# Top-k attention and two MLPs on one core: queries loaded and x transposed once per visit, and a newly searched order

## The chip, the core and the metric

The kernel runs on one core of a Trainium2 chip. A core has five engines, each with its own instruction queue that is worked off in order: TensorE (PE) for matmuls, VectorE (DVE), ScalarE (ACT), GpSimd (POOL) and SyncE (SP), which here issues all DMA transfers; these run on 16 DMA engines that the core shares out among all transfers. The metric is the time of one execution in device microseconds; the median of some runs counts.

## The reference

Four batches of eight heads, 576 positions of 64 values. Attention keeps, for each query, the 32 largest scores; its output goes through two MLPs with 2048 hidden units.

```python
scores = scale * np.matmul(q, k.transpose(0, 1, 3, 2))
kth = np.partition(scores, -32, axis=-1)[..., -32:-31]
scores = np.where(scores >= kth, scores, -1e9)
attn = softmax(scores)                       # with 1e-9 added to the sum
x = matmul(attn, v) as (4 * 576) x 512
h = x @ moe_w_in;   y = softplus(h) @ moe_w_out
h = y @ moe2_w_in;  out = (h - np.tanh(h)) @ moe2_w_out
```

(softplus is written out in the reference as max(h, 0) + log1p(exp(-|h|)).)

## The kernel before, in words

**Numbers.** Everything that PE multiplies is split into two 16-bit halves, a high and a low one, and a product is three matmuls (high by high, high by low, low by high). So every operand is made by ACT (cast to the high half) and POOL or DVE (difference, the low half).

**Visits and tiles.** Attention goes by visits: a visit is one batch, one pair of heads and two of the four blocks of 128 query positions (`PLAN`, line 32). There are 32 visits. Each has four full tiles of 128 queries by 576 keys (two heads by two blocks), kind "n". In every second group of visits a fifth tile holds the 64 left-over queries of both heads, kind "l". That makes 128 full and 16 left-over tiles.

A visit's preparation: `visit_load` (line 1219) loads queries to `qraw`, keys to `kraw`, values to `v`, and the left-over queries to `ql`; `visit_prep_q` (1290) scales the queries, splits them into `qhl` and has a DMA transpose them into `qT`; `visit_prep_left` (1306) does this for the left-over queries through a zeroed buffer `zq`, in which each head has its own block, into `qlT`. Keys and values of a visit that comes again are stored as split operands to DRAM (`kd`, `vd`) and loaded from there.

A tile's way: `front` (1341) multiplies queries and keys on PE into PSUM (`s`), ACT copies that to `ssb`; DVE runs four MAX8 and three MATCH_REPLACE8 to find the 32 largest; ACT (exponential) and DVE or ACT (mask) make `x`, the unnormalized probabilities; ACT and POOL split them to `hl`; a DMA transposes these to `pT`; `back` (1442) multiplies them with the values on PE into `px`, ACT scales by the reciprocal sum into `x32`. When both heads of one block of queries are there, ACT casts `x32` to the high half in `xs`, POOL makes the low half, and a DMA transposes `xs` into the chunk's tile `xy`, the input of the first MLP.

**MLPs.** Four visits (the eight heads of two blocks) fill a chunk of 256 positions; there are eight of these, and two of 128 for the left-over positions. `mlp_step` does one eighth of an MLP for a chunk: PE makes `h` from `xy` and the weights, ACT, POOL and DVE make `g`, PE adds to `y`. The weights (names `whi`, `wlo`; the number behind tells which) are loaded as raw 32-bit words in pieces of 1 MB or 256 KB, partly into the places of later weights or free `xy` tiles, and converted by ACT, DVE and POOL during the first 200 us.

**What sets the order.** The kernel's functions only record operations. A planner (`Recorder.order`, line 570) then lays them out: it starts from ranks with random noise (`SEED`, `SIG`), plays the program through with prices for every operation (`price`, 340, `place`, 462), and adds the entries of the table `SHIFTS`, each of which moves operations of some engines in a stretch of time by random or fixed amounts. The order that comes out is what each engine's queue holds. For PE gaps that it foresees it adds matmuls without use (`idle`, 607), 128x256, in the trace at line 677. All recorded operations are issued from line 680, so the trace shows them all under that line.

**Buffers.** `al(tag, n, ...)` hands out n buffers of a name in turn: `NQT` = 2 for `qT`, `NXS` = 3 for `xs` (one block of queries each), `NX32` = 2 for `x32`, `NXX` = 3 for DVE's `x`, `NQR` = 1 for `qraw`.

Of the kernel before, what the change touches and what calls it, by code (L numbers as in the profile page):

```python
# [35 lines left out]
NQT = 2  # L36
NHL = 1
XE = 1
# [4 lines left out]
NOWN = 8  # L43
# [29 lines left out]
NXS = 3  # L73
# [5 lines left out]
SEED = 3785  # L79
# [5 lines left out]
SIG = 60  # L85
# [10 lines left out]
NXX = 3  # L96
# [25 lines left out]
PTC = 1600.0  # L122
SPC = 640.0

SHIFTS = (
# [6 lines left out]
    (9776, 35155, 55155, 400, "A"), (63973, 103704, 123704, 400, "PDAGS"), (27296, 1008651, 1068651, 1000, "PDAGS"),  # L132
# [8 lines left out]
    (75800, 448312, 508312, 100, "PDAGS"), (73125, 179938, 219938, 400, "PD"), (19493, 716429, 756429, 200, "PDAGS"),  # L141
    (72577, 458633, 518633, 200, "G"), (91158, 95592, 115592, 1000, "G"), (38484, 434008, 442008, 6000, "G"), (63646, 482912, 522912, 100, "A"),
    (52951, 193726, 213726, 200, "PDAGS"), (90708, 836742, 896742, 400, "A"), (72979, 149882, 157882, 200, "PDAGS"),
# [540 lines left out]
def topk_attention_two_mlps(  # L684
# [81 lines left out]
    def with_table(out, in_, func, **kw):  # L766
        op = nc.scalar.activation(out, in_, func, **kw)
        nc.after(op, table[0])
        table[1].append(op)

    zq = al("zq", 1, [P, 2, 2, 2, D], F16)
    nc.gpsimd.memset(zq, 0.0)


    tiles_ = al("tiny", 1, [P, 176 if OWN < 99 else 120], F32)
    used_ = [0]

    def tiny(n=1):
# [663 lines left out]
    def back(st):  # L1442
# [38 lines left out]
        if st is not it.sts[-1]:  # L1481
            return
# [487 lines left out]
```

## Time and profile before

| | us |
|---|---|
| median of three runs | 1121.09 (1120.64 to 1122.13) |
| profiled execution | 1124.62 |
| its span | 1122.9 |
| PE busy | 1000.7 (89%) |
| DVE busy | 929.0 (83%) |
| ACT busy | 904.3 (81%) |
| POOL busy | 776.6 (69%) |

The span is what the profiler saw between the first and the last instruction; 1.7 us of the profiled execution lie around it. Busy shares are means over stages that differ: PE's granted clock, for example, is at half speed for some of the time between 80 and 190 us and full from 200 us on, so the same matmul has two durations. Matmul records overlap, since matmuls are pipelined: the step from one to the next is shorter than the duration shown.

### The profile page before, as it was taken

How to read it: one execution, taken by the hardware profiler on the slowest of the kernel's cores; microseconds unless marked ns; L12 is line 12 of the kernel's file. 1: busy time of each engine (PE TensorE's matmuls, PEld its weight loads, DVE VectorE, ACT ScalarE, POOL GpSimd, SP SyncE). 2: the span in 40 equal slices, each digit the busy share in tenths (PEclk: the TensorE clock that was granted, in tenths of full speed). 3: DMA queues.
4: the chain of work that ended last, by engine and by line, in shares of the span. 5: the costliest groups of instructions: out<-in, count | busy, mean ns of one | idle time of the engine just before them, and what ended most of it. 6: DMA issues, size and time to landing. Idle time of an engine off the chain costs nothing.

```text
span 1122.9 us, 27775 instructions
## 1 busy us (share of the span) xinstructions
PE 1000.7 (89%) x9994; PEld 784.6 (70%) x9994; DVE 929.0 (83%) x2059; ACT 904.3 (81%) x1873; POOL 776.6 (69%) x1185
## 2 busy tenths in 40 slices
PE   2437645989999899999999999999999999999998
PEld 1323334877678767876799868976787789968965
DVE  4987899989999999999999999999999899410111
ACT  5987999899998998888999898998988777633422
POOL 5794246999889667768788676788876657543433
PEclk9998855999999999999999999999999999999999
DMA  9999999547777886556887755577566363200000
GB/s 255 292 256 269 292 250 225 124 129 143 139 151 187 166 169 146 86 97 126 191 183 136 140 116 104 78 124 166 131 122 107 72 117 61 52 4 20 1 11 19
DMA packets 323130, 153.13 MB, mean 136 GB/s; under 512 B 270256, under 2 KB 314288, under 8 KB 322992
## 3 DMA queue, kind: packets, MB, share of 16 engines
q1 hardware_dynamic: 322992, 151.36, 62.7%
q8 instruction: 78, 1.28, 0.5%
q14 instruction: 60, 0.49, 0.2%
HBM read 73.01 MB, written 15.37 MB: 79 GB/s over the span
## 4 chain that ended last, share of the span: by engine, by line
PE 55%; DVE 18%; POOL 7%; ACT 7%; DMA 6%; issue 6%; SPq 2%; POOLq 0%; ACTq 0%; DVEq 0%
PE h L680 24%; PE y L680 24%; DVE x L680 7%; DVE m L680 7%; PE px L680 4%; PE s L680 3%; SPq L680 2%; POOL hl L680 2%; DMA pT<-hl 2%; ACT ssb L680 1%; POOL wlo L680 1%; ACT x L680 1%; DMA kraw<-in_k_dram 1%; DVE xy L680 1%; DVE wlo L680 1%
## 5 line engine op out<-in xcount | busy, mean ns | idle before, releaser
L680 PEld LDWEIGHTS <-whi 128*128 128x128 f16 (+1 forms) x3994 | 372.6, 99 | 78.3 <-DVE whi L680 14.4
L680 PE MATMUL h<-xy,whi 128*128 128x256 f16 (+1 forms) x2560 | 395.6, 263 | 1.5 <-DVE xy L680 0.6
L680 PE MATMUL h<-xy,wlo 128*128 128x256 f16 (+1 forms) x1280 | 325.0, 263 | 0.0
L680 DVE MAX8 m<-x 128x8 f32<-128x576 f32 x432 | 314.5, 746 | 0.9
L680 POOL TENSOR_TENSOR hl<-x,hl 128x64 f16<-128x64 f32 (+1 forms) x288 | 213.1, 757 | 82.8 <-ACT hl L680 62.1
L680 PEld LDWEIGHTS <-wlo 128*128 128x128 f16 (+1 forms) x1986 | 195.3, 99 | 34.2 <-issue 8.1
L680 DVE MATCH_REPLACE8 x<-m,x 128x576 f32<-128x576 f32 x288 | 213.9, 744 | 0.0
L680 PE MATMUL y<-g,whi 128*128 128x256 f16 (+1 forms) x1280 | 198.9, 262 | 1.1 <-POOL g L680 1.1
L680 PE MATMUL y<-whi,g 128*128 128x512 f16 x576 | 193.7, 379 | 0.3 <-POOL g L680 0.3
L680 POOL TENSOR_TENSOR g<-r,g 128x512 f16<-128x512 f32 (+1 forms) x160 | 173.4, 1084 | 20.3 <-PE y L680 11.3
L680 PE MATMUL y<-g,wlo 128*128 128x256 f16 (+1 forms) x640 | 162.3, 262 | 0.0
L680 DVE SCALAR_TENSOR_TENSOR r<-h,hinb,r 128x512 f32<-128x512 f32 (+1 forms) x80 | 54.8, 687 | 115.8 <-ACT r L680 115.4
L680 PEld LDWEIGHTS <-g 128*128 128x128 f16 x864 | 81.6, 98 | 74.5 <-POOL g L680 1.4
L680 ACT ACTIVATE x<-ssb,nb,tiny 128x576 f32<-128x576 f32 x136 | 117.4, 865 | 5.6 <-DVE m L680 2.9
L680 PEld LDWEIGHTS <-pT 128*128 128x128 f16 (+1 forms) x2240 | 89.6, 102 | 46.1 <-issue 22.4
L680 DVE MAX8 m<-ssb 128x8 f32<-128x576 f32 x144 | 107.6, 747 | 14.9 <-ACT ssb L680 14.5
L680 PE MATMUL px<-vhl,pT 128*128 128x65 f16 (+1 forms) x2240 | 96.8, 197 | 24.9 <-ACT x L680 12.1
L680 PE MATMUL s<-kT,qT 128*128 128x288 f16 x512 | 91.7, 306 | 20.9 <-ACT ssb L680 11.5
L680 PE MATMUL y<-wlo,g 128*128 128x512 f16 x288 | 109.1, 379 | 0.0
L680 DVE MATCH_REPLACE8 x<-m,ssb 128x576 f32<-128x576 f32 x144 | 106.5, 740 | 0.0
L680 ACT CAST hl<-x 128x576 f16<-128x576 f32 x144 | 96.5, 670 | 3.7 <-DMA pT<-hl 3.4
L680 ACT COPY ssb<-s 128x576 f32<-128x576 f32 x144 | 91.2, 633 | 4.8 <-PE s L680 4.1
(154 smaller groups left out, 1597.5 us busy)
## 6 DMA issues: line engine op xcount, KB each, us to landing
whi<-in_moe_w_in_dram SPq DMA_DIRECT2D x11, 1023.0 KB, 6.5
whi<-in_moe_w_out_dram SPq DMA_DIRECT2D x7, 1023.5 KB, 7.2
vd<-vhl SPq DMA_DIRECT2D x16, 330.0 KB, 3.8
vhl<-vd SPq DMA_DIRECT2D x16, 330.0 KB, 3.5
kd<-kT SPq DMA_DIRECT2D x32, 160.0 KB, 2.3
kT<-kd SPq DMA_DIRECT2D x32, 160.0 KB, 2.9
xy<-in_moe_w_out_dram SPq DMA_DIRECT2D x18, 255.8 KB, 3.4
qraw<-in_q_dram SPq DMA_DIRECT2D x64, 64.0 KB, 2.6
```

The source lines that it names most:

```text
L680: fn(*a, **k)
```

## The change

- `visit_load`: the queries of both heads of a visit come in one transfer.
- `visit_prep_left`: the left-over queries lie in `zq` without the zero blocks; one cast and one subtraction on 128 rows instead of two each on 64 rows, and the transpose is half as long. `front` reads the smaller `qlT`.
- `back`: `xs` and `x32` hold both blocks of queries of a visit; one cast, one subtraction and one transpose per visit, after its last full tile.
- Buffers: `NQT` 2 to 1, `NXS` 3 to 1 (twice as large), `NX32` 2 (twice as large), `NXX` 3 to 4, `NOWN` 8 to 2.
- Planner: a plain transfer's time is its bytes by 300 instead of 330 per ns; new `SEED` and `SIG`, and a new table `SHIFTS` with 206 entries instead of 264.
- Branches that no setting used are taken out.

```diff
-NQT = 2
+NQT = 1
...
-NXS = 3
+NXS = 1
...
-SEED = 3785
+SEED = 1322
...
-SIG = 60
+SIG = 25.0
...
-NXX = 3
+NXX = 4
...
 SHIFTS = (
-    (86484, 682077, 832077, 6000, "G"), (43207, 851448, 891448, 6000, "S"), (65683, 300726, 308726, 400, "PDAGS"),
...
+    (14983, 315778, 335778, 1000, "A"), (37653, 130389, 150389, 6000, "G"), (79820, 1004060, 1154060, 2500, "PDAGS"),
...
-            return (770.0 if kb == 32 else 690.0 if kb == 16 else 550.0 if kb in (230, 232) else SPC), size / 330.0
+            return (770.0 if kb == 32 else 690.0 if kb == 16 else 550.0 if kb in (230, 232) else SPC), size / 300.0
...
-            for j in range(2):
-                nc.sync.dma_start(
-                    vi.q[:, j],
-                    q[b, h0 + j, 0 : NB * P, :].rearrange("(p t) d -> p t d", t=NB)[:, ts[0] : ts[0] + nt, :],
-                )
+            nc.sync.dma_start(
+                vi.q,
+                q[b, h0 : h0 + 2, 0 : NB * P, :].rearrange("h (p t) d -> p h t d", t=NB)[:, :, ts[0] : ts[0] + nt, :],
+            )
...
-        for j in range(2):
-            r = slice(j * SL, (j + 1) * SL)
-            f = vi.ql[r, :].unsqueeze(1).to_broadcast([SL, 2, D])
-            nc.scalar.copy(zq[r, 0, j], f)
-            nc.gpsimd.tensor_sub(zq[r, 1, j], f, zq[r, 0, j])
-        vi.qlT = al("qlT", 1, [P, 2, 2, P], F16)
...
+        f = vi.ql.unsqueeze(1).to_broadcast([P, 2, D])
+        nc.scalar.copy(zq[:, 0], f)
+        nc.gpsimd.tensor_sub(zq[:, 1], f, zq[:, 0])
+        vi.qlT = al("qlT", 1, [P, 2, P], F16)
+        nc.sync.dma_start_transpose(out=vi.qlT, in_=zq.rearrange("p r u d -> p (r u d)"))
...
-        if st is it.sts[0]:
-            it.x = al("xs", NXS, [P, 2, P], F16)
...
+        if st is it.sts[0] and it is it.all[0]:
+            x = al("xs", NXS, [P, 2, nt, P], F16, cap=2 * P)
+            x32 = al("x32", NX32, [P, nt, P], F32, cap=2 * P)
...
-        if st is not it.sts[-1]:
+        if st is not it.sts[-1] or it is not it.all[-1]:
             return
...
+        nc.scalar.copy(hi, x32)
+        nc.gpsimd.tensor_sub(lo, x32, hi)
...
+        nc.sync.dma_start_transpose(out=to, in_=it.x[0:rows].rearrange("p r i c -> p (r i c)"))
```

What the order becomes is seen best at three places. In the rows, a name is a tile with its number, `out<-in` and the shape. The line number is that of the recorder's call, 680 before and 667 after the change.

The first place is SP's queue ahead of the last transposes of x that the first chunk (`xy_0_125`, `xy_0_126`) needs. Before:

```order
L680 DMA qraw_75<-in_q_dram 128x128 x2
L680 DMA_TRANSPOSE qT_86<-qhl_85 128x8x128
L680 DMA whi_0_71<-in_moe_w_out_dram 128x2x2047
L680 DMA_TRANSPOSE xy_0_126<-xs_128 128x2x128
L680 DMA vhl_138<-vd_139 128x1320
L680 DMA_TRANSPOSE pT_121<-hl_120 128x9x128
L680 DMA wlo_0_72<-in_moe_w_out_dram 128x1023
L680 DMA xy_0_98<-in_moe_w_out_dram 128x1023
L680 DMA_TRANSPOSE xy_0_126<-xs_135 128x2x128
```

After:

```order
L667 DMA qraw_75<-in_q_dram 128x2x128
L667 DMA kT_113<-kd_115 128x640
L667 DMA_TRANSPOSE qlT_147<-zq_63 128x2x128
L667 DMA kT_81<-kd_139 128x640
L667 DMA_TRANSPOSE pT_120<-hl_119 128x9x128
L667 DMA wlo_0_72<-in_moe_w_out_dram 128x1023
L667 DMA_TRANSPOSE xy_0_126<-xs_128 128x4x128
L667 DMA_TRANSPOSE pT_124<-hl_123 128x9x128
L667 DMA whi_0_71<-in_moe_w_out_dram 128x2x2047
```

Two transposes of 128x2x128 have become one of 128x4x128, and a 1 MB load of weights (`whi_0_71`, 128x2x2047), ahead of them before, now stands behind. The query load is one row instead of two.

The second place is ACT's queue at the same point of the program. Before:

```order
L680 ACTIVATE whi_0_69<-whi_0_71,tiny_64 128x1024
L680 ACTIVATE x_0_129<-px_127,r_2_140 128x64
L680 CAST wlo_0_72<-xy_0_96 128x256
L680 CAST xs_128<-x_0_129 128x128
L680 CAST wlo_0_72<-xy_0_97 128x256
L680 ACTIVATE px_134,ss_88<-px_134 128x128
L680 CAST wlo_0_68<-y_78 128x512
L680 ACTIVATE r_0_130<-px_127,tiny_64 128x1
L680 ACTIVATE ssb_94<-ssb_94,m_109 128x576
L680 ACTIVATE x_1_136<-px_127,r_0_130 128x64
L680 ACTIVATE x_110<-ssb_94,nb_117,tiny_64 128x576
L680 CAST xs_135<-x_1_136 128x128
```

After:

```order
L667 CAST hl_119<-x_93 128x576
L667 ACTIVATE r_0_130<-px_127,tiny_64 128x1
L667 ACTIVATE x_110<-ssb_111,nb_121,tiny_64 128x576
L667 CAST wlo_0_72<-xy_0_96 128x256
L667 CAST wlo_0_72<-xy_0_133 128x256
L667 ACTIVATE x_1_141<-px_127,r_0_130 128x64
L667 ACTIVATE px_134,ss_108<-px_134 128x128
L667 ACTIVATE whi_0_69<-whi_0_71,tiny_64 128x1024
L667 CAST xs_128<-x_1_141 128x256
L667 CAST hl_123<-x_110 128x576
L667 ACTIVATE whi_0_69<-whi_0_71,tiny_64 128x1024
```

The casts of `xs` are one of 128x256 instead of two of 128x128; the cast of weights from `y` (`wlo_0_68<-y_78`) that stood between them comes later, and the split of one tile's probabilities more (`hl_119<-x_93`) stands ahead.

The third place is SP's queue where the queries of the visit after the 28th are transposed to `qT`, late in the program. Before:

```order
L680 DMA kd_217<-kT_81 128x640
L680 DMA out_dram<-r_158 128x512
L680 DMA v_74<-in_v_dram 128x2x256
L680 DMA vd_216<-vhl_103 128x1320
L680 DMA_TRANSPOSE qT_86<-qhl_85 128x8x128
L680 DMA_TRANSPOSE pT_124<-hl_123 128x9x128
L680 DMA v_74<-in_v_dram 64x2x64 x2
L680 DMA_TRANSPOSE pT_121<-hl_120 128x9x128
L680 DMA_TRANSPOSE xy_0_100<-xs_128 128x2x128
```

After:

```order
L667 DMA_TRANSPOSE xy_0_132<-xs_128 128x2x64
L667 DMA vd_217<-vhl_136 128x1320
L667 DMA_TRANSPOSE pT_124<-hl_123 128x9x128
L667 DMA_TRANSPOSE pT_120<-hl_119 128x9x128
L667 DMA_TRANSPOSE qT_86<-qhl_85 128x8x128
L667 DMA kT_81<-kd_207 128x640
L667 DMA kT_83<-kd_209 128x640
L667 DMA vhl_103<-vd_208 128x1320
L667 DMA_TRANSPOSE pT_124<-hl_123 128x9x128
```

Before, the transposes of queries go to `qT_86` and `qT_116` in turn; after, all go to `qT_86`, which the tiles of the visit ahead are still reading, so this row now waits for the last score of that visit, and two transposes of probabilities (`pT`) and a store of values stand right ahead of it.

## Rows read from the trace of the kernel before

**Rows 1.** The page: span, busy time by engine, PE's busy tenths in 40 slices

```profile
span 1122.9 us, 27775 instructions
...
PE 1000.7 (89%) x9994; PEld 784.6 (70%) x9994; DVE 929.0 (83%) x2059; ACT 904.3 (81%) x1873; POOL 776.6 (69%) x1185
...
PE   2437645989999899999999999999999999999998
```

**Rows 2.** Timeline of PE: start, duration, operation (the first chunk's first matmul)

```profile
188.35 0.60 PE L680 MATMUL h<-xy,whi 128*128 128x256 f16 x2
```

**Rows 3.** Busy time by engine in stretches; then PE clock, DMA share, GB/s

```profile
0.00:188.35 188.35, 90.87 (x626) 58.33 (x627) 153.47 (x356) 161.57 (x329) 108.45 (x156) 0.84 1.03 262
188.35:270.00 81.65, 73.59 (x729) 62.82 (x728) 78.01 (x170) 74.98 (x171) 77.02 (x123) 0.97 0.59 139
270.00:500.00 230.00, 221.69 (x2265) 175.61 (x2264) 226.81 (x513) 209.45 (x449) 175.67 (x272) 1.00 0.73 145
```

**Rows 4.** The same stretches, the planner's matmuls without use alone (line 677; PE, PEld)

```profile
188.35:270.00 81.65, 8.31 (x64) 6.06 (x64) 0.97 0.59 139
270.00:500.00 230.00, 5.61 (x43) 4.11 (x43) 1.00 0.73 145
```

**Rows 5.** Waits of ACT and DVE before 188.35 us: total us, times, longest

```profile
ACT wlo L680 <- DMA whi<-in_moe_w_in_dram: 7.4, 3, 4.1
ACT wlo L680 <- DMA wlo<-in_moe_w_out_dram: 4.9, 1, 4.9
...
DVE whi L680 <- ACT wlo L680: 15.5, 5, 10.7
```

**Rows 6.** Timeline of SP: start, time of issuing, transfer

```profile
171.96 0.81 SPq L680 DMA_DIRECT2D qraw<-in_q_dram  x2
174.05 1.24 SPq L680 DMA_TRANSPOSE qT<-qhl  x1
```

**Rows 7.** DMA issues: count, KB each, median us from issue to landing

```profile
qraw<-in_q_dram SPq DMA_DIRECT2D x64, 64.0 KB, 2.6
...
xy<-xs SPq DMA_TRANSPOSE x80, 2.4
...
qT<-qhl SPq DMA_TRANSPOSE x32, 3.3
out_dram<-r SPq DMA_DIRECT2D x4, 128.0 KB, 2.4
qlT<-zq SPq DMA_TRANSPOSE x16, 2.6
```

**Rows 8.** Groups by operation and shape: busy us, mean ns of one | idle before

```profile
L680 ACT CAST qhl<-qraw 128x512 f16<-128x512 f32 x32 | 19.7, 616 | 0.4 <-DMA qT<-qhl 0.3
L680 ACT CAST xs<-x 128x128 f16<-128x128 f32 x64 | 18.8, 301 | 0.3
...
L680 ACT CAST zq<-ql 64x128 f16<-64x128 f32 x32 | 9.4, 295 | 0.5
...
L680 POOL TENSOR_TENSOR xs<-x,xs 128x128 f16<-128x128 f32 x64 | 28.0, 439 | 19.5 <-ACT xs L680 19.0
...
L680 POOL TENSOR_TENSOR g<-r,g 128x256 f16<-128x256 f32 x32 | 21.4, 673 | 1.3
...
L680 POOL TENSOR_TENSOR zq<-ql,zq 64x128 f16<-64x128 f32 x32 | 14.2, 443 | 5.1 <-ACT zq L680 3.5
```

**Rows 9.** What the DMA engines moved from 0 to 188.35 us

```profile
DMA packets 60466, 49.44 MB, mean 262 GB/s; under 512 B 39968, under 2 KB 57379, under 8 KB 60451
```

**Rows 10.** Groups of ACT from 188.35 to 270 us

```profile
L680 ACT CAST zq<-ql 64x128 f16<-64x128 f32 x4 | 1.2, 300 | 0.1
L680 ACT CAST xs<-x 128x128 f16<-128x128 f32 x3 | 0.9, 292 | 0.0
```

**Rows 11.** Timeline of PE at full clock: start, duration, operation

```profile
197.58 0.38 PE L680 MATMUL h<-xy,whi 128*128 128x256 f16 x2
...
197.91 0.38 PE L680 MATMUL h<-xy,whi 128*128 128x256 f16 x2
```

More of the change, by code (lines that the diff above doesn't have):

```diff
@@ L42 @@
 OWN = 2
-NOWN = 8
+NOWN = 2
 OWN0 = 0
@@ L769, in with_table @@
         table[1].append(op)
-    zq = al("zq", 1, [P, 2, 2, 2, D], F16)
-    nc.gpsimd.memset(zq, 0.0)
-    tiles_ = al("tiny", 1, [P, 176 if OWN < 99 else 120], F32)
+    zq = al("zq", 1, [P, 2, 2, D], F16)
+    tiles_ = al("tiny", 1, [P, 164 if OWN < 99 else 120], F32)
     used_ = [0]
@@ L1198, in topk_attention_two_mlps @@
             else:
-                c = NG * GW - 2 * 2 * (NB + 1) * D * p
+                c = (NG - 1) * GW - 2 * 2 * (NB + 1) * D * p
                 x = wlo[2][:, c : c + 2 * 2 * (NB + 1) * D].bitcast(F32).rearrange("p (h t d) -> p h t d", h=2, t=NB + 1)
@@ L1346, in front @@
             prods = []
[L1347 to L1349 removed]
         ps = al("s", 1, [P, 2, 512], F32, pb)
[L1351 to L1372 removed]
         with nc.burst():
[L1374 removed]
+            if st.kind == "l":
                 for hf in range(2):
@@ L1378, in front @@
                             c = slice(j * SL, (j + 1) * SL)
-                            nc.tensor.matmul(ps[c, hf, 0:HS], vi.qlT[:, r, j, c], vi.kT[j][:, hf * HS : (hf + 1) * HS],
+                            nc.tensor.matmul(ps[c, hf, 0:HS], vi.qlT[:, r, c], vi.kT[j][:, hf * HS : (hf + 1) * HS],
                                              start=(r == 0), stop=(r == 1))
-                prods = []
-            for hf in range(2):
+            for hf in range(2 if prods else 0):
                 for i, (lhs, rhs) in enumerate(prods):
@@ L1458, in back @@
                 nc.tensor.matmul(o, st.pT[:, NB, c0:c1], vl[:, NB, 0 : D + 1], start=False, stop=True)
-        if st is it.sts[0]:
-            it.x = al("xs", NXS, [P, 2, P], F16)
-            if XE:
-                it.x32 = al("x32", NX32, [P, P], F32)
+        nt = len(it.all)
+        if st is it.sts[0] and it is it.all[0]:
+            x = al("xs", NXS, [P, 2, nt, P], F16, cap=2 * P)
+            x32 = al("x32", NX32, [P, nt, P], F32, cap=2 * P)
+            for u, i in enumerate(it.all):
+                i.x, i.x32, i.one = x, x32, x32[:, u, :]
         rows = P if st.kind == "n" else SL
@@ L1475, in back @@
             sc, src = r[0:rows, i : i + 1], o[:, 0:D]
-            if XE:
-                nc.scalar.activation(it.x32[0:rows, c], src, AF.Copy, scale=sc)
-            else:
-                nc.scalar.activation(it.x[0:rows, 0, c], src, AF.Copy, scale=sc)
-                nc.vector.scalar_tensor_tensor(it.x[0:rows, 1, c], src, sc, it.x[0:rows, 0, c], op0=ALU.mult, op1=ALU.subtract)
-        if st is not it.sts[-1]:
-            return
-        if XE:
-            if XE == 1:
-                nc.scalar.copy(it.x[0:rows, 0, :], it.x32[0:rows])
-            else:
-                nc.vector.tensor_copy(it.x[0:rows, 0, :], it.x32[0:rows])
-            nc.gpsimd.tensor_sub(it.x[0:rows, 1, :], it.x32[0:rows], it.x[0:rows, 0, :])
-        nc.sync.dma_start_transpose(
-            out=it.chunk.x.block(vi.p)[:, :, it.col : it.col + rows],
-            in_=it.x[0:rows].rearrange("p r c -> p (r c)"),
-        )
+            nc.scalar.activation(it.one[0:rows, c], src, AF.Copy, scale=sc)
+        if st is not it.sts[-1] or it is not it.all[-1]:
+            return
+        hi, lo = (it.x[0:rows, u].rearrange("p i c -> p (i c)") for u in range(2))
+        x32 = it.x32[0:rows].rearrange("p i c -> p (i c)")
+        nc.scalar.copy(hi, x32)
+        nc.gpsimd.tensor_sub(lo, x32, hi)
+        to = it.chunk.x.block(vi.p)
+        if st.kind == "n":
+            to = to[:, :, it.all[0].col : it.col + P].rearrange("p r (i c) -> p (r i) c", c=P)
+        else:
+            to = to[:, :, it.col : it.col + rows]
+        nc.sync.dma_start_transpose(out=to, in_=it.x[0:rows].rearrange("p r i c -> p (r i c)"))
     class Halves:
@@ L1714, in topk_attention_two_mlps @@
                 its.append(it)
+                it.all = its
             for h in range(2):
@@ L1723, in topk_attention_two_mlps @@
                     it.spec, it.chunk, it.col, it.sts = vspec, lc, (ch.b % 2) * SL, []
+                    it.all = [it]
                     st = ST()
```

45 lines of the change are left out of this document (9 added, 36 removed), and 118 rows, old and new, of the table SHIFTS.

## The prediction

> **What bounds the kernel now.** I read the page first, then cut the span into stages. The page gives the matrix engine (PE) 1000.7 us of the 1122.9 us span [rows 1], so only 122.2 us are open to any reordering, and the change takes no matmul away. The slices say where these lie: PE is at 2 to 7 tenths in the first seven slices and at 9 from slice 11 on [rows 1].
>
> The cut that matters is the first matmul of the first MLP on attention output, which starts at 188.35 us [rows 2]. I call it the MLP start. The windows [rows 3] give PE's idle time as window minus busy: 97.5 us before 188.35; 8.1 us from there to 270; 8.3 us to 500; what is left of the 122.2 us, 8.3 us, lies in the 623 us after that. To this belong the keep-warm matmuls that the planner puts into foreseen gaps: 8.3 us from 188.35 to 270 and 5.6 us from 270 to 500 [rows 4]; these count as busy but are of no use. So: 97.5 us before the MLP start, 30.3 us of idle and filler time (8.1 + 8.3 + 8.3 + 5.6) between it and 500, and nearly nothing later. From 500 on PE sets the time, and an edit that only makes ACT, POOL or the queues lighter there is worth nothing.
>
> Before the MLP start no single engine is full: DVE is busy 153.5 of 188.35 us, ACT 161.6, the DMA engines show a share of 1.03 at 262 GB/s [rows 3]. ACT's idle time there is ended mostly by weight loads (7.4 and 4.9 us in the two largest rows), DVE's by ACT (15.5 us in the largest) [rows 5]. The chain reads: load, ACT, DVE, and the load end is where the supply is exhausted.
>
> **The change part by part.**
>
> *Queries in one load.* 64 loads of 64 KB become 32 of 128 KB, same bytes. An issue costs SP about 0.4 us (0.81 us for two [rows 6]), so 32 × 0.4 = 12.8 us of SP. SP is not on the path for long stretches, so I take 0. Landing: 2.6 us for 64 KB; the nearest row for 128 KB is an output store with 2.4 us [rows 7]. So the landing changes by some tenths either way, and the load is issued long before its use, while the tiles of the visit ahead are worked on; without that cover it would be a tenth of a us or two per visit.
>
> *One transpose of x per visit.* 64 transposes of two blocks become 32 of four. SP saves 32 issues of about 1.24 us, the price of the transposes of queries [rows 6], again off the path. A four-block transpose is in the trace already, for the left-over queries: 2.6 us against 2.4 us for two blocks [rows 7]. The MLP start needs both tiles of a visit anyway, so merging costs it 0.2 us. On ACT, 64 casts of 301 ns [rows 8] become 32 of 128x256. No such form is there; between 301 ns for 128 columns and 616 ns for 512 [rows 8] a straight line gives 406 ns (bounds: the two ends). Saved: 64 × 0.301 − 32 × 0.406 = 6.3 us. On POOL, 439 ns for 128 columns and 673 ns for 256 [rows 8] give 64 × 0.439 − 32 × 0.673 = 6.6 us.
>
> *Left-over queries without the zero block.* 32 ACT casts of 295 ns on 64 rows become 16 on 128 rows, priced as the 301 ns cast: 4.6 us; on POOL 32 × 0.443 − 16 × 0.439 = 7.2 us [rows 8]. ACT is spared 10.9 us in all and POOL 13.8 us, spread over the span; only what falls before 500 us counts.
>
> *Term 1, the MLP start.* The order shows what stands in each queue ahead of the last transpose that the first chunk needs. DVE: 281 rows in both; one more first replacement, two more others and two more maxima (5 × 0.75 + 3 loads of match values) against two 1.3 us weight subtractions and three small rows: +0.5 us. ACT: the edits save 8 × 0.301 − 4 × 0.406 + 4 × 0.295 − 2 × 0.301 = 1.4 us, and what is moved past the point saves another 0.5 us: −1.9 us. SP and DMA: a 1 MB weight load, one 0.26 MB load, and one 0.26 MB transpose stand behind this point instead of ahead of it, two 0.16 MB reloads of keys ahead instead of behind: by shapes 47.75 MB instead of 48.99 MB, which agrees with the 49.44 MB moved by 188.35 us [rows 9]. At 262 GB/s 1.24 MB is 4.7 us. Gains do not add on parallel chains: all 4.7 us if the transfers set the start, at most 1.9 us if ACT does, nothing if DVE does. I take 3.3 us, midway between the first two, because the chain begins at the loads but ACT is the busiest engine.
>
> *Term 2, 188 to 270 us.* ACT is busy 75.0 and POOL 77.0 of 81.65 us [rows 3] and PE starves between them. Three x casts and four left-over casts on ACT lie in the stretch [rows 10]. A merged pair of x casts saves 0.196 us on ACT and 0.205 on POOL, a left-over pair 0.289 and 0.447, so ACT is spared 1.5 × 0.196 + 2 × 0.289 = 0.9 us and POOL 1.5 × 0.205 + 2 × 0.447 = 1.2 us, both on the path there: −1.0 us. *Term 3, 270 to 500 us.* ACT's 10.9 us, spread over the span of 1123 us, give 2.2 us for these 230 us, where ACT is at 91% [rows 3]; the rest of its waits are not PE's, so I take somewhat under half: −1.0 us (bounds 0 and −2.2).
>
> *Term 4, one buffer for transposed queries.* This is the only added wait. The next visit's queries may be transposed only when the last full tile of the present visit has been scored; SP stands still on that PE wait (by its listed waits in 26 of 32 cases; a wait on PE stood there in 16 before, for a buffer two visits old), with probability transposes queued behind it. Then PE waits for 1.24 us of issue [rows 6] plus 3.3 us of landing [rows 7], 4.5 us, unless it has work between. From the order, with 0.33 us for three 256-column matmuls [rows 11] and the other forms by their columns, the work between the two scores is under 4.5 us at three of the 27 boundaries after the MLP start: 4.4, 4.0 and 2.0 us. That is 0.1 + 0.5 + 2.5 = 3.1 us if nothing else holds PE there and every transpose goes out at once. I take +1.5 us, bounds 0 and 17 (below).
>
> A fourth x buffer on DVE removes no large wait: the largest that ends DVE's idle time is ACT's weight cast [rows 5], not a buffer. I take 0. The changed rate in the planner (it makes a plain transfer longer, 300 for 330 bytes per ns) and the new tables work only through the order.
>
> The sum is −3.3 − 1.0 − 1.0 + 1.5 = −3.8 us: span 1119.1 us, profiled execution 1124.62 − 3.8 = 1120.8 us, and since the median of the runs shown is 1121.09 us, 3.5 us under the profiled one, 1117.3, say **1117 us**.
>
> **The rivals.** *No net change.* Occupancy of the transfers need not be a bound; then term 1 is at most ACT's 1.9 us, and with DVE's 0.5 us of extra work and the longer transpose it nearly vanishes, while term 4 eats terms 2 and 3: 1119 to 1123 us, likeliest 1121. The share of 1.03 speaks against it, DVE's 95% from 188 to 270 us [rows 3] for it: an earlier start meets a second chunk that comes no earlier. The Trainium skill states this side as a rule ("Perfetto Trace Analysis", Identifying the Most-Contended Engine): transfers are to be judged by HBM utilization, not by the engines' occupancy. By that rule 262 GB/s is no bound, term 1 falls to ACT's share, and the sum to −2.4 us or less; no row here settles it. The same page (DMA Optimizations) says that splitting transfers lets some start sooner, which speaks against both merges; the rows price that at 0.2 us.
>
> *Slower, by the single query buffer.* If the transposes leave SP 3 us late on the average, held by what stands ahead in that queue, PE needs 7.5 us of work at each boundary, and eight of the 27 have less (4.4, 5.0, 6.2, 4.0, 7.4, 6.6, 2.0, 7.1): 17.3 us lost, −5.3 + 17.3 = +12 us, 1133 us. At 1.5 us late four fall short, 8.6 us, 1124 us. It decides from about 1.3 us of lateness. For it: SP's queue is in order, and PE is so full after 500 us that any stall is paid in full. Against it: the order leaves 8 us or more at most boundaries. Likeliest 1126.
>
> *A larger gain.* If the new order lets ACT wait less for loads (12.3 us in two rows [rows 5]) and the start comes 8 us earlier, and half of the 16.4 us of idle and filler time from 188 to 270 us goes too, it is −16 us, 1105 us; with half of both, 1113. Against it: the order holds 110 fillers instead of 108, so the planner sees as many gaps as before.
>
> **How the numbers follow.** About 0.2%, 2.2 us, is what a measurement can tell from no change. Forecast (1112 to 1118.8): 0.42. Larger gain (1103 to 1112): 0.13. No change: 0.19. Slower (1123.4 to 1133): 0.26. So faster 0.55, same 0.19, slower 0.26. The range of 8 in 10 leaves a tenth or less on either side: 1107 to 1128.
>
> **What would show it.** Term 1: the first h<-xy matmul at 185 us (183.6 to 188) and some 1.2 MB less moved by then. Terms 2 and 3: ACT near 893 us, POOL near 763 us, and idle and filler time from the start to start + 312 us at 28 us instead of 30. Term 4: PE or its weight loads waiting for qT<-qhl after 200 us, 1 to 3 us in all; over 8 us and the slower case has come. A start after 190 us, or PE under 9 tenths after slice 20, would make the forecast wrong.

## The result and the profile after

The changed kernel takes 1112.51 us (median of 4 runs, 1109.65 to 1113.47). Its ratio to the kernel before is 0.9912, 95% interval 0.9890 to 0.9933, so 0.9% faster: about 9 us, where 4 us were forecast. The profiled execution took 1111.59 us, the span in it is 1109.9 us. The page of after, against [rows 1]:

```profile
span 1109.9 us, 27484 instructions
...
PE 998.6 (90%) x9996; PEld 785.7 (71%) x9996; DVE 928.0 (84%) x2059; ACT 898.2 (81%) x1825; POOL 769.7 (69%) x1136
...
PE   2446749989889999999999999999999999999998
```

The engines' sums have hardly moved: PE 2.1 us less, DVE 1.0, ACT 6.1, POOL 6.9. The span of the profiled execution is 13.0 us shorter. Part of that is the profiled execution of before, which lies 3.5 us above its median; the one of after lies 0.9 us under its own.

The gain has one place. The timeline of PE (start, duration, operation) has the MLP start, the first product of the first MLP, here, where [rows 2] had 188.35:

```profile
172.24 0.63 PE L667 MATMUL h<-xy,whi 128*128 128x256 f16 x2
```

It comes 16.1 us earlier, and 3.1 us of that are given back by the end (16.1 − 13.0). One profiled execution of each kernel stands behind these numbers. By the medians the gain is 9 us and not 13, and where in the span the 4 us between the two belong isn't known. The windows, cut at the start, 81.66 us and 230 us behind it as in [rows 3], show both. The columns are PE, PEld, DVE, ACT, POOL busy, then PE's granted clock, the DMA share and GB/s:

```profile
0.00:172.24 172.24, 87.15 (x622) 56.63 (x623) 152.67 (x352) 156.94 (x316) 105.70 (x144) 0.88 1.05 279
172.24:253.90 81.66, 75.47 (x725) 64.14 (x724) 76.28 (x177) 76.55 (x168) 79.03 (x119) 0.96 0.55 144
253.90:483.90 230.00, 217.83 (x2210) 172.23 (x2209) 221.93 (x496) 204.40 (x430) 171.95 (x261) 0.99 0.69 145
483.90:1109.90 626.00, 618.18 (x6445) 492.71 (x6442) 477.17 (x1038) 460.30 (x914) 413.02 (x614) 1.00 0.47 94
```

Read the DVE column of the first line, the third of the five. DVE does the same work before the start as before (152.67 us against 153.47), but in 172.24 us and not in 188.35. Its idle time there fell from 34.9 to 19.6 us, which is 15.3 of the 16.1 us. The waits of DVE before the start (total us, times, longest) say which idle time went. First those of before that [rows 5] does not show, then those of after:

```profile
DVE m L680 <- ACT ssb L680: 6.8, 4, 2.8
DVE wlo L680 <- ACT wlo L680: 5.7, 2, 4.5
```

```profile
DVE whi L667 <- ACT wlo L667: 12.2, 3, 10.0
...
DVE m L667 <- ACT ssb L667: 1.2, 3, 0.7
DVE wlo L667 <- ACT wlo L667: 1.2, 1, 1.2
```

DVE waits for ACT 13.4 us less in these three groups: 3.3 and 4.5 for casts of weights (the rows of `whi` and `wlo`), 5.6 for copies of scores. ACT, in turn, stood before weight loads for 15.5 us: the 12.3 us of [rows 5] and a third row. After, one group of such waits is left; the wait of 4.9 us for a W_out load is gone:

```profile
ACT wlo L680 <- DMA whi<-in_moe_w_out_dram: 3.2, 3, 1.4
```

```profile
ACT wlo L667 <- DMA whi<-in_moe_w_in_dram: 6.2, 2, 4.7
```

Sums of waits don't say which wait made which; the order of time does. One place in the kernel before can be followed from a load to DVE (start, duration, operation; the bracket: idle time before it, and what ended it):

```profile
88.12 1.33 ACT L680 CAST wlo<-wlo 128x1024 f16<-128x1024 bf16 x1 [4.89 <-DMA wlo<-in_moe_w_out_dram]
89.48 1.23 DVE L680 SCALAR_TENSOR_TENSOR wlo<-wlo 128x1024 int32<-128x1024 int32 x1 [4.54 <-ACT wlo L680]
```

ACT stands before a load that hasn't landed, and DVE, next in line, before ACT's cast: 4.5 of the 15.3 us. The longest wait for a copy of scores has another cause. PE had waited for transposed keys, so the scores themselves came late:

```profile
77.90 1.12 PE L680 MATMUL s<-kT,qT 128*128 128x288 f16 x4 [4.56 <-DMA kT<-khl]
79.72 0.76 DVE L680 MAX8 m<-ssb 128x8 f32<-128x576 f32 x1 [2.78 <-ACT ssb L680]
```

So late loads are one cause among several of the idle time that went.

Behind the start nothing is gained in these two executions. The planner's keep-warm matmuls (line 664 now, against [rows 4]; PE and PEld) in the two stretches:

```profile
172.24:253.90 81.66, 9.65 (x76) 7.27 (x76) 0.96 0.55 144
253.90:483.90 230.00, 4.94 (x25) 2.61 (x25) 0.99 0.69 145
```

Idle and filler time of PE in the 312 us behind the start is 6.2 + 12.2 + 9.7 + 4.9 = 33.0 us; it was 30.3.

### The profile page after: what moved, and what is told of

The parts are those of the page before. It is cut to its first block, busy times and chain, and to the rows that moved or that the text cites. A ratio compares the mean times of both kernels' runs of the same rounds, so it can differ in the third digit from the quotient of the medians.

```text
span 1109.9 us, 27484 instructions
## 1 busy us (share of the span) xinstructions
PE 998.6 (90%) x9996; PEld 785.7 (71%) x9996; DVE 928.0 (84%) x2059; ACT 898.2 (81%) x1825; POOL 769.7 (69%) x1136
## 4 chain that ended last, share of the span: by engine, by line
PE 58%; DVE 15%; ACT 10%; POOL 7%; issue 5%; DMA 4%; SPq 0%; ACTq 0%; POOLq 0%; DVEq 0%
PE h L667 26%; PE y L667 24%; DVE m L667 6%; DVE x L667 5%; PE px L667 4%; PE s L667 4%; ACT ssb L667 2%; ACT x L667 2%; POOL hl L667 2%; POOL wlo L667 1%; ACT wlo L667 1%; ACT whi L667 1%; DMA pT<-hl 1%; ACT hl L667 1%; ACT r L667 1%
## 5 line engine op out<-in xcount | busy, mean ns | idle before, releaser
L667 POOL TENSOR_TENSOR hl<-x,hl 128x512 f16<-128x512 f32 (+1 forms) x288 | 217.3, 771 | 77.5 <-ACT hl L667 63.5
L667 PEld LDWEIGHTS <-wlo 128*128 128x128 f16 (+1 forms) x1986 | 195.4, 99 | 39.1 <-DVE wlo L667 11.8
L667 DVE MAX8 m<-ssb 128x8 f32<-128x576 f32 x144 | 107.3, 745 | 10.7 <-ACT ssb L667 10.0
L667 POOL TENSOR_SCALAR r<-r,gsb 128x512 f32<-128x512 f32 (+1 forms) x80 | 52.6, 658 | 66.3 <-ACT g L667 65.8
```

Of the source, the lines that this page charges most:

```text
L667: fn(*a, **k)
```

## The experiments

All fourteen kernels in one table. "Start" is the first product of the first MLP, "DVE" its busy and idle time before that, GB/s the rate of the transfers there, "behind" the span less the start. The ratios are to the kernel before, which ran beside each with medians of 1120.97 to 1122.20 us; differences between two ratios are good to some 0.3%, 3 us. The changed kernel itself did not run beside the experiments. The columns from "start" on are of one profiled execution each.

| kernel | ratio to before, 95% | median us | start | DVE busy, idle | GB/s | behind |
|---|---|---|---|---|---|---|
| before | 1 | 1121.09 | 188.35 | 153.5, 34.9 | 262 | 934.6 |
| changed | 0.9912 (0.9890 to 0.9933) | 1112.51 | 172.24 | 152.7, 19.6 | 279 | 937.7 |
| forms_undone | 1.0017 (1.0002 to 1.0032) | 1122.02 | 172.51 | 153.5, 19.0 | 278 | 946.9 |
| xs_undone | 0.9986 (0.9967 to 1.0005) | 1120.05 | 173.21 | 153.3, 19.9 | 277 | 944.7 |
| q_undone | 0.9939 (0.9916 to 0.9962) | 1114.54 | 172.41 | 152.2, 20.2 | 279 | 941.4 |
| max_twice | 0.9991 (0.9970 to 1.0012) | 1119.12 | 177.67 | 159.0, 18.7 | 271 | 939.1 |
| early330 | 0.9983 (0.9968 to 0.9997) | 1120.80 | 179.09 | 152.7, 26.4 | 268 | 940.4 |
| search330 | 1.0002 (0.9982 to 1.0022) | 1120.70 | 176.63 | 151.5, 25.1 | 271 | 941.8 |
| x3 | 1.0296 (1.0269 to 1.0323) | 1153.39 | 178.19 | 154.9, 23.3 | 270 | 974.8 |
| x3_again | 1.0045 (1.0026 to 1.0064) | 1126.87 | 176.19 | 154.5, 21.7 | 273 | 947.9 |
| early300 | 1.0071 (1.0053 to 1.0089) | 1129.91 | 195.33 | 156.2, 39.1 | 254 | 930.9 |
| before_search300 | 1.0089 (1.0065 to 1.0112) | 1131.63 | 181.91 | 154.6, 27.4 | 263 | 948.3 |
| order_only | 1.0547 (1.0519 to 1.0575) | 1180.87 | 187.10 | 154.5, 32.6 | 257 | 994.7 |
| old_order | 1.1038 (1.1008 to 1.1068) | 1236.03 | 191.91 | 153.8, 38.2 | 256 | 1038.8 |

The theories at the outset: A, the searched order closes VectorE's gaps before the start; B, the merged instructions do it by lighter engines, as the terms of the prediction have it; C, the fourth x buffer does it.

In most of these kernels the planner's order is replaced by a stored place for every step; a step is issued at its place, or as soon behind it as all that it depends on has been issued:

```diff
-            done = self.order(margin)
+            done = self.given()
```

### forms_undone: the three merged forms taken apart, order kept

Each pair is recorded as one step, so that it keeps its place in the order. The lines that do this are left out here, and so is the order of the dimensions of `xs`, which follows the pairs:

```diff
-            nc.sync.dma_start(vi.q, q[b, h0 : h0 + 2, ...])
+            for j in range(2):
+                nc.sync.dma_start(vi.q[:, j], q[b, h0 + j, ...])
...
-        nc.scalar.copy(hi, x32)
-        nc.gpsimd.tensor_sub(lo, x32, hi)
-        nc.sync.dma_start_transpose(out=to, in_=it.x[0:rows].rearrange("p r i c -> p (r i c)"))
+        for u in range(nt):
+            nc.scalar.copy(it.x[0:rows, u, 0], it.x32[0:rows, u])
+        for u in range(nt):
+            nc.gpsimd.tensor_sub(it.x[0:rows, u, 1], it.x32[0:rows, u], it.x[0:rows, u, 0])
+        for u, i in enumerate(it.all):
+            nc.sync.dma_start_transpose(out=to[:, :, i.col : i.col + rows], in_=it.x[0:rows, u].rearrange("p r c -> p (r c)"))
...
-        nc.scalar.copy(zq[:, 0], f)
-        nc.gpsimd.tensor_sub(zq[:, 1], f, zq[:, 0])
+        for r in half:
+            nc.scalar.copy(zq[r, 0], f[r])
+        for r in half:
+            nc.gpsimd.tensor_sub(zq[r, 1], f[r], zq[r, 0])
```

> The changed kernel with its order, its four x buffers and its single qT and xs buffers kept step for step, but the three merged forms taken apart again where they stand: two loads of queries per visit, two casts, two subtractions and two transposes of x per visit, two casts and two subtractions of the leftover queries. Theory A (the searched order closes VectorE's gaps before the first W_in product; the forms weigh little): MLP start within 2 us of 172.2 us, time within 2 us of 1112.5. Theory B (the lighter ScalarE, GpSimd and DMA queue do it, the terms of the prediction): MLP start 3 to 16 us later, 175.5 to 188 us, and the time up by 3 us or more. Theory C (the fourth x buffer): no change, 1112.5.

The start did not move (172.51 us), which speaks against B as a theory of the start. Yet the whole gain is gone, 1122.02 us. B had a time like this, but none of the theories had a loss behind an unmoved start. The windows of this kernel (columns as above):

```profile
172.51:254.17 81.66, 74.23 (x707) 62.68 (x706) 75.22 (x172) 75.66 (x167) 77.20 (x119) 0.95 0.54 138
254.17:484.17 230.00, 215.48 (x2170) 168.55 (x2167) 217.98 (x489) 203.31 (x438) 173.95 (x273) 0.99 0.71 145
484.17:1119.40 635.23, 625.01 (x6507) 497.36 (x6505) 478.94 (x1050) 468.14 (x949) 422.76 (x643) 1.00 0.49 93
```

Behind the start PE needs 946.9 us and not 937.7: 6.0 us more idle time (32.2 against 26.2) and 3.2 us more busy time. PE issues the same instructions in the same order in both, so they can be set side by side. Of the 3840 products `h<-xy` the 251st comes 2.3 us later than in the changed kernel, the 501st 4.9, the 1251st 7.0, the 2001st (at 715 us) 10.0, the last 9.5: a loss in small pieces up to some 700 us, and none behind that. Among PE's waits behind 172 us the one for the transposed probabilities grew most, from the first line (the changed kernel) to the second (this one):

```profile
PE px L667 <- DMA pT<-hl: 2.4, 4, 0.8
```

```profile
PE px L1119 <- DMA pT<-hl: 6.5, 8, 1.5
```

### xs_undone and q_undone: one of the forms each

The edits are the second part of the diff above (xs_undone) and the first (q_undone).

> The changed kernel in its order, with the x step of a visit taken apart again: two casts, two subtractions and two transposes back to back instead of one each (32 more instructions on ScalarE, GpSimd and the DMA queue each). All three forms apart cost 9.5 us behind an unchanged start. If the transposes are what costs (each is a long issue on the queue, and the pT transposes behind it come later): 6 us or more of the 9.5, near 1119. If ScalarE and GpSimd time by itself costs, 32 times some 0.1 us each: 1 to 3 us, 1114 to 1115. MLP start within 1 us of 172.2 in both.

> The changed kernel in its order, with the load of queries of a visit taken apart into two again (32 more issues on the DMA queue, no other engine). If issues on the queue cost by themselves (32 times some 0.6 us, of which a part delays a transpose behind): 3 us or more, 1115 to 1119. If only the transposes and casts of x cost: within 1 us of 1112.5. MLP start within 1 us of 172.2.

The x step costs 0.74% when undone (0.9986 against 0.9912), about 8 us; the load of queries 0.27%, 3 us, which is as large as the uncertainty and decides between neither of its expectations. The 8 us are in the range that was expected if the transposes cost, not in the 1 to 3 us for ScalarE's and GpSimd's own time; over the whole span ACT is busy 1.2 us more than in the changed kernel (899.4 against 898.2) and POOL 2.0 (771.7 against 769.7). That the transposes' issues are the cause is still not shown: casts, subtractions and transposes were undone together. Behind 172 us PE's matmuls wait for pT nearly as before (2.8 against 2.4 us) and for ScalarE's score copies more (11.2 against 7.8 us). But PE also waits in its weight loads of `pT`. With these counted, the wait for transposed probabilities grows from kernel to kernel. In the views of `pT` from 172 us on, this line reads, for the changed kernel, q_undone, xs_undone and forms_undone (us, times):

```profile
  DMA pT<-hl: 5.7, 8
  DMA pT<-hl: 8.0, 11
  DMA pT<-hl: 9.9, 15
  DMA pT<-hl: 17.2, 21
```

These transposes stand in the same queue as the added issues, so this fits the transposes' side; waits of weight loads can overlap matmuls, and not all of them are lost time.

### max_twice: does DVE set the start now?

Shortened; the two maxima are one step of the order:

```diff
-            return lambda: nc.vector.max(m[:, 8 * i : 8 * i + 8], src)
+            for _ in range(2 if i == 0 and 1 <= st.i <= 12 else 1):
+                nc.vector.max(m[:, 8 * i : 8 * i + 8], src)
```

> The changed kernel in its order, with the first row maximum of twelve of the sixteen score tiles ahead of the first W_in product taken twice (12 more VectorE instructions of 0.74 us, 8.9 us in all, nothing else). If VectorE's own work with its few gaps sets the MLP start now: start 7 to 9 us later, 179 to 181 us, and the time up by 5 to 9 us. If bytes, ScalarE or the loads set it (the terms of the prediction): the start moves by 3 us or less.

```profile
0.00:177.67 177.67, 89.67 (x622) 57.28 (x623) 159.02 (x364) 158.70 (x316) 106.51 (x144) 0.88 1.03 271
```

Twelve more maxima make DVE 6.4 us busier before the start, the start comes 5.4 us later, and the median 6.6 us (9 us by the ratios). That lies between the two expectations (7 to 9 us, 3 us or less), nearer to the first. So DVE with its gaps sets the start for the greater part. It is not the fullest engine there: ACT is busy 156.9 of the 172.24 us of the changed kernel and DVE 152.7. No run added work to ACT, so whether ACT sets the start as much is not known. The stretch behind the start is 1.5 us longer than in the changed kernel: the shift isn't made up for by the end.

### early330: the old price of transfers, up to the start

Theory D: the planner of before, at 330 bytes per ns, puts ScalarE's casts ahead of loads that land later on the chip. Here only the steps ahead of the first product are laid out anew, with the changed kernel's priorities and the old price; each engine passes over a step whose transfer has not landed by the plan.

> The changed kernel with its instructions and buffers; only the order of the steps up to the first W_in product is laid out again with the old price of transfers (330 bytes per ns), behind it the order of the changed kernel. Theory D: loads land later than this order assumes, MLP start at 174 to 182 us instead of 172, time 1114 to 1121. Rival (price is of no weight, buffers and instructions are): start within 2 us of 172, time within 2 us of 1112.5.

```profile
ACT wlo L1108 <- DMA whi<-in_moe_w_in_dram: 6.5, 3, 3.6
ACT wlo L1108 <- DMA whi<-in_moe_w_out_dram: 4.6, 3, 2.5
```

```profile
DVE whi L1108 <- ACT wlo L1108: 12.3, 5, 9.0
DVE m L1108 <- ACT ssb L1108: 7.6, 6, 3.5
```

Start and time are as D expected: 6.9 us later, and 0.7%, 8 us, slower. ACT's waits for weight loads are back from 6.2 to 11.1 us, and DVE's wait for score copies from 1.2 to 7.6 us. But most of the second did not come from the first. The two longest of DVE's waits for score copies, 5.7 of the 7.6 us, in order of time:

```profile
52.72 1.14 PE L1108 MATMUL s<-kT,qT 128*128 128x288 f16 x4 [2.00 <-DMA qT<-qhl]
54.64 0.76 DVE L1108 MAX8 m<-ssb 128x8 f32<-128x576 f32 x1 [3.54 <-ACT ssb L1108]
...
96.26 0.58 ACT L1108 CAST wlo<-h 128x512 f16<-128x512 f32 x1 [1.50 <-PE h L1108]
101.51 0.76 DVE L1108 MAX8 m<-ssb 128x8 f32<-128x576 f32 x1 [2.19 <-ACT ssb L1108]
```

At 54.64 the scores came late, because PE had waited for transposed queries. At 101.51 ACT had waited for PE, and then had other work ahead of the copy. Neither stands right behind a late load. So the run shows that, with the same instructions and buffers, the order ahead of the start alone is worth 8 us and works through DVE's idle time (26.4 against 19.6 us). It doesn't show theory D's mechanism. Nor does it show that the price is the reason: the same laying out at 300 was not run for the changed kernel, so the way of laying out may itself cost what was lost.

### early300: the new price in the kernel before, up to the start

The same with the kernel before and its own priorities.

> The kernel before, with its own instructions and buffers. Only the order of the steps up to the first W_in product is laid out again: the same priorities as before, each engine passing over a step whose transfer, priced at 300 bytes per ns in place of 330, has not landed; nothing is searched, and behind the first W_in product the order is that of before. Theory D (before loses its time where ScalarE, in order, stands before a load that lands later than its plan assumed: 7.4 us for three W_in loads and 4.9 us for one W_out load before the start, and VectorE behind it): MLP start at 172 to 179 us instead of 188, ScalarE's waits for weight loads before the start down from 12.3 to under 7 us, time 1107 to 1115. Rival (the earlier start needs the fourth x buffer or the new instructions): start at 184 us or later, time 1118 or more.

The start came later, 195.33 us, and not earlier. The timeline of PE (the bracket: idle time before it, and what ended it) shows why:

```profile
180.95 1.11 PE L1125 MATMUL px<-whi 128*128 128x128 bf16 x8 [6.17 <-DVE whi L1125]
...
194.40 1.11 PE L1125 MATMUL px<-whi 128*128 128x128 bf16 x8 [7.07 <-DVE whi L1125]
195.33 0.61 PE L1125 MATMUL h<-xy,whi 128*128 128x256 f16 x2
```

In the new early order W_out conversions were further behind, and the order of before, taken up at the cut, has them ahead of the first product. PE waits 13.2 us for them. ACT's waits for weight loads did not fall to under 7 us either, they are 16.7. So the cut spoiled the test: it says nothing on the price, only that a product of weights (`px<-whi`) in PE's queue can hold the first product.

### before_search300 and search330: price and search

Theory E: with the price of 300 the search finds the better order by itself. Both kernels have an order searched on by random shifts of priorities that are kept where the planner's end falls. The edit is the price, and a new table of priorities; below for before_search300, in search330 the price changes the other way:

```diff
-            return (770.0 if kb == 32 else 690.0 if kb == 16 else 550.0 if kb in (230, 232) else SPC), size / 330.0
+            return (770.0 if kb == 32 else 690.0 if kb == 16 else 550.0 if kb in (230, 232) else SPC), size / 300.0
```

> The kernel before, with its own instructions, three x buffers and two qT buffers. Its planner prices transfers at 300 bytes per ns in place of 330, and its order is searched on from that of before (random shifts of priorities, kept where the planner's end falls; a shorter search than an order of this kind had). Theory E (price and search carry the gain, forms and buffers little): MLP start at 172 to 178 us, time 1110 to 1116. Rival F (the order can only be this tight with the merged forms, which cost 9.5 us where they were undone, and the fourth x buffer): start may come earlier than 188, but the time stays at 1117 or more.

> The changed kernel's instructions and buffers, the old price of 330 bytes per ns in the planner, and an order searched on at that price from that of the changed kernel, until the planner's end was lower than that of the changed kernel. Theory E (at 330 the search puts steps ahead of loads that land later on the chip): start at 176 us or later, ScalarE's waits for loads before the start over 9 us instead of 6.2, time 1116 to 1123. Rival (the price is of no weight once the order is searched): 1108 to 1113.

The first falls on the rival's side: the start comes 6.4 us earlier than in before (181.91), the time is 0.9% longer than before. Price and search alone do not bring the gain with the old instructions and buffers, by this search. It went on from the order of before and kept what the planner's end rewarded, and yet the kernel became slower: at the size of the gain, the planner's end was no measure of the time here. The second kernel, with all new instructions and buffers, the old price and another order, has the start (176.63) and the time that E had, 1120.70 us, no faster than before (1.0002); ACT's waits for loads of weights are 8.4 us, a little under E's 9. But x3_again below, searched at the new price, is no faster either. So search330 shows that all the other edits, without this very order, are worth nothing measurable, and not that the price is the reason.

### x3 and x3_again: the fourth x buffer

```diff
-NXX = 4
+NXX = 3
```

x3 keeps the order of the changed kernel; x3_again has one searched on for three buffers.

> The changed kernel with three x buffers instead of four and its order otherwise kept (some 40 of VectorE's rows come later because their buffer is still held). Theory A (order): MLP start within 3 us of 172.2, time 1112 to 1115. Theory B (forms): the same, 1112.5. Theory C (the fourth x buffer lets VectorE go on with another tile while it would wait): VectorE idle before the start back from 19 to over 30 us, start over 182 us, time 1119 or more.

> The changed kernel with three x buffers and an order searched on for three from that of the changed kernel, price 300. With the order of four kept, three buffers cost 41 us. Theory G (most of that is an order that doesn't fit): 1113 to 1121, start at 172 to 177 us. Rival H (the fourth buffer itself is worth it, VectorE waits for GpSimd to release an x tile in any order): 1130 or more, and VectorE's waits for x behind GpSimd at 10 us or more between 172 and 600 us.

With the order kept, three buffers cost 41 us, of which 6 us lie ahead of the start and the rest behind it. C's time came, but not at C's place: the start is 178.19 and not over 182, DVE's idle time before it 23.3 and not over 30 us. DVE's waits from 172 to 600 us, the changed kernel and x3:

```profile
DVE x L667 <- POOL hl L667: 1.0, 1, 1.0
```

```profile
DVE x L1119 <- POOL hl L1119: 16.7, 18, 2.1
```

DVE stands before the next tile until GpSimd has released an x tile, 18 times. Searched for three buffers, that wait goes and the loss shrinks to 1.3% (1.0045 against 0.9912), 15 us, inside neither expectation (up to 1121; 1130 or more). So about two thirds of the 41 us was an order that didn't fit. The 15 us are no sure price of the buffer either: the kernel before, with three x buffers, the old instructions and its larger `qT` and `xs` buffers, is 0.45% faster than x3_again. Whether a longer search would take the rest isn't known.

### order_only and old_order: order and kernel exchanged

order_only is the kernel before in the order of the changed one, old_order the changed kernel in the order of before.

> The kernel before, with its own instructions, three x buffers, two qT and three xs buffers, but issued in the order of the changed kernel (each step at the place of its counterpart; where a buffer is missing a step comes as early as its buffer allows, which moves some 50 of VectorE's 1611 rows). Theory A (order): MLP start at 172 to 176 us, time 1112 to 1115, most of the 9 us gained. Theory B (forms): start at 185 to 188 us, time near 1121. Theory C (the fourth x buffer): start at 182 to 188 us, time 1118 to 1121.

> The changed kernel's instructions and buffers, issued in the order of the kernel before (merged steps at the place of the second of the two that they replace). Theory A (order): MLP start at 184 to 188 us and time 1118 to 1122, the gain is gone. Theory B (forms): start at 172 to 178 us, time 1112 to 1117. Theory C (the fourth x buffer): it can't help in an order made for three, 1118 to 1122. The prediction's own sum of terms without an order that fills gaps: start at 185, time 1117.

All theories missed both by far, 60 and 115 us slower than before. Neither part is worth anything with the other's counterpart. In old_order one reason can be read from ACT's waits (whole span):

```profile
ACT qhl L1122 <- DMA qT<-qhl: 64.1, 18, 4.8
...
ACT xs L1122 <- DMA xy<-xs: 21.7, 9, 5.0
```

An order made for two qT buffers and three xs buffers casts the next queries early. With one buffer their transpose waits for PE, ACT's next cast into qhl waits for that transpose, and all that is queued behind it on ACT waits too, DVE's and PE's supply among it. This is the single query buffer of the prediction's slower case, but mostly by another way: PE and its weight loads wait 12.6 us for `qT` here, ACT 64.1. How much of the 115 us it makes is not worked out. In the changed kernel's own order ACT's wait is 2.8 us. The tile's view (who waited for qT: us, times):

```profile
who waited for it (us, times):
  ACT qhl L667: 2.8, 3
  ACT ssb L667: 1.5, 5
  PEld L667: 1.5, 2
  PE s L667: 0.4, 1
```

## Why the prediction was right in direction and too small

**Term 1, the start: the right place, 16.1 us for 3.3.** The step that failed is the choice of what sets the start. It was priced by bytes over a rate (4.7 us) and by ACT's row count (1.9 us), "nothing if DVE does". The bytes were right: 48.14 MB moved by the start, 1.3 MB less than [rows 9], forecast 1.2. The rate of 262 GB/s was no ceiling: it became 279 at a share of 1.05, and over the fourteen kernels it goes from 254 to 279 at shares of 0.96 to 1.05, high where the start is early. In max_twice, where only DVE got more work, the start came later and the rate fell to 271: there it followed the start. The Trainium skill ("Perfetto Trace Analysis", Identifying the Most-Contended Engine) has transfers judged by HBM utilization and not by the engines' occupancy; the traces agree in that the rate went from 262 to 279 GB/s at nearly one share (1.03 and 1.05).

In the table DVE's busy time before the start is 151 to 156 us in every kernel but max_twice, whatever the start, so the start moves with DVE's idle time. That alone would not single DVE out: ACT's busy time is 157 to 164 us in all fourteen, and it too lost idle time (26.8 to 15.3 us) besides 4.6 us of work. What singles DVE out is max_twice. [rows 3] had the idle time: DVE is busy 153.47 of 188.35. I counted DVE's rows, found them equal, and stopped; the other 34.9 us were the term. An order that changes none of an engine's work can still take its waits away, and the upper bound of Term 1 should have been those waits: 34.9 us less the 10.7 for the first weights [rows 5], some 24.

The larger gain, given 0.13, had part of the mechanism: "ACT wait less for loads", start 8 us earlier. ACT's waits for weight loads before the start fell from 15.5 to 6.2 us, and over the other kernels they are 4 to 8 us where the start is at 172 to 178 and 11 to 17 where it is later, but for order_only (5.8 us, start at 187.10). So they go with the start, and other waits make it too. The argument against the larger gain, that the planner places as many fillers as before (110 for 108), did not bear on it: fillers stand in gaps of PE that the planner foresees, and what went was idle time of DVE.

That 1112.51 us lies within 1107 to 1128 is luck as far as the sum goes. By the profiles its terms are −16.1, +2.7 (for the −2.0 of terms 2 and 3) and near nothing (for +1.5), −13.4 in all and not −3.8. The range held because it was made wide enough for the rivals; the time lies half a us inside the stretch given to the forecast (1112 to 1118.8), next to that of the larger gain.

**Terms 2 and 3, lighter ACT and POOL: −2 forecast, not seen in the sum.** Idle and filler time went up by 2.7 us where it should have gone down by 2. At an unchanged order the forms are worth much more than 2 us: 9.2 us of span behind the start in forms_undone. Both can hold if the order of before fitted the old forms as well as the new one fits the new: its stretch behind the start is no longer (934.6 against 937.7). That is a reading, and no run tests it. The engines' groups, against [rows 8] and [rows 7]:

```profile
L667 POOL TENSOR_TENSOR xs<-x,xs 128x256 f16<-128x256 f32 x32 | 22.6, 706 | 10.1 <-ACT xs L667 9.8
...
L667 ACT CAST xs<-x 128x256 f16<-128x256 f32 x32 | 13.0, 406 | 0.3
...
L667 POOL TENSOR_TENSOR zq<-ql,zq 128x128 f16<-128x128 f32 x16 | 6.8, 426 | 0.2
...
L667 ACT CAST zq<-ql 128x128 f16<-128x128 f32 x16 | 4.8, 301 | 0.3 <-DMA qlT<-zq 0.3
```

```profile
qraw<-in_q_dram SPq DMA_DIRECT2D x32, 128.0 KB, 3.4
...
xy<-xs SPq DMA_TRANSPOSE x48, 2.6
```

ACT's durations were right (406 and 301 ns). POOL's was 5% low (706 for 673), and the 128 KB load lands after 3.4 us, not 2.4. ACT's total fell by 6.1 us instead of the 10.9 forecast. The step that was mis-sized is the price of a merged pair on ACT: durations overlap, so they don't add. Where another instruction follows directly, it begins 189 ns after a cast of 128 columns (median of 46 of the 64 in the kernel before) and 295 ns after one of 256 (24 of 32), so a merged pair saves some 83 ns and not 196. With 2.7 us for 32 pairs and 4.6 for the left-over queries (9.4 to 4.8) that is 7.3 us. POOL's total fell by 6.9 us instead of 13.8. Its two groups spare 12.8 (28.0 to 22.6 and 14.2 to 6.8), but the low halves of the probabilities (`hl`) took 217.3 us for 213.1; the rest is spread over other groups.

**Term 4, the single qT buffer: +1.5 forecast, near nothing found.** PE waits for qT 0.4 us and its weight loads 1.5 us in the whole span, ACT 2.8 us. The order keeps clear of it. That such an order matters shows in old_order, where ACT waits 64.1 us.

**The fourth x buffer: 0 forecast, wrong for this order.** "Removes no large wait" was read from a trace whose order had been made for three buffers; DVE waits only 1.9 us for GpSimd's x in it between 172 and 600 us. The new order can't do without the buffer: 41 us, and with an order searched for three, as far as that search went, 15.

**The rivals.** No net change and slower are out by the result. That the change is a matter of its order was right in words ("work only through the order") and had no price in the sum.

A small misreading without weight in the sum: PE isn't at 9 tenths from slice 11 on, slice 14 of [rows 1] has 8.

**What stays open.** The gain belongs to the set: forms, buffers and order together. Shown are the place (DVE's gaps before the start, with max_twice), one place where such a gap comes from a late load by way of ACT (4.5 us), and that the order ahead of the start alone is worth 8 us (early330). What was taken back by itself cost 0.7% or more of the time, where 0.9% was gained: the three forms, the x step, the fourth x buffer, the order; the loads of queries cost 0.27%. Not taken back by themselves were the zero blocks of the left-over queries and the smaller buffers for `qT` and `xs`. Not settled is how much another, longer search would find for any one of the sets, and so whether the buffers, the forms or only a lucky search made this order possible.

## What to carry to other kernels

Where the order is searched, an edit is not to be priced by the waits in the old trace alone: that trace shows little waiting for a resource which its order was made to fit. For a stretch with a steady amount of work on each engine, take the busy time of the full engines as the floor and their waits as what a new order can win, and find out by added work (max_twice) which of them sets the pace. Bytes over the mean rate is a bound only if the rate is shown not to rise. Two sums of waits that grow together don't show that one made the other: follow single waits in order of time (early330). When one part of a co-tuned set is to be tested, lay out the order for the rest again, or the run measures the misfit (x3: 41 us, 15 after a new search; old_order: 115 us).

## What was unexpected

A cast or a subtraction on 128 partitions costs the same as on 64: the left-over queries' cast 301 ns on 128 rows and 295 ns on 64 [rows 8], the subtraction 426 and 443 ns. Merging two halves of the partitions is worth a whole instruction.

Casts that follow each other directly overlap: in forms_undone 64 casts of 128 columns, in pairs and each 300 ns long, fill only 15.8 us, so a pair costs 494 ns against 406 ns for one cast of 256 columns. The merge saves 88 ns there, not the 196 that their single durations promise; it is the same where the two stood apart, as the steps above show.

```profile
L1119 ACT CAST xs<-x 128x128 f16<-128x128 f32 x64 | 15.8, 300 | 0.1
```
